# Chunk ends sent with K's transfers, a step fused, the exponential table first, weights held three pieces ahead, the first groups reordered

## The chip, the cores and the metric

The kernel runs on one core of a Trainium2 chip. The metric is the device time of one execution in microseconds (us). Three runs of the kernel before took 955.64, 958.70 and 959.11 us, median 958.7. Further down, TensorE (PE) multiplies matrices, VectorE (DVE) and ScalarE (ACT) do the elementwise work, and SyncE (SP) issues all DMA transfers, one after the other, from one queue.

## The reference

Three parts follow each other. The first is a linear attention with complex decay, for 4 batches, 8 heads, 768 steps and 48 dimensions:

```
scale = min(|a|, 0.999) / (|a| + 1e-6);  a = a * scale          # a complex, per step and dimension
for t in range(S):
    S_re, S_im = a[t] * (S_re + i S_im);  S_re += outer(k[t], v[t])
    y[t] = q[t] @ S_re
```

The second and third work on the 3,072 tokens of y, with 384 columns each:

```
h = x @ w_in;  x2 = (h * clip(h + 3, 0, 6) / 6) @ w_out         # 384 -> 2048 -> 384
out = (((x2 @ w1) * (x2 @ w2)) @ w3) @ w_out2                   # 384 -> 1024 -> 1024 -> 384
```

The weights come as 64-bit numbers, and are turned into 32-bit ones on the chip.

## The kernel before

The sequence is cut into chunks of 128 steps, 6 in a batch, 24 in all. Two chunks make a group, and `group(gi)` does for a group what doesn't need the state: from a_re and a_im (tiles ar and ai, 128x768) the logarithm of the magnitude and the angle; a running product of the magnitudes within a chunk (L534, into s, called G in the code) and a running sum of the angles (L540, into ai, called th); then sine and cosine of the angle (tile cs), and K and Q multiplied by them (Kc, and cs again). In that layout a dimension lies across partitions and heads together, so six DMAs bring Kc into KT and six bring cs into QT, 96 partitions of one head each (L584). `chunk(u)` transposes Kc on TensorE (L634, into Ks by ScalarE copies), updates the state A (L669), forms the scores (L643), masks them on VectorE (into P), and multiplies them with v and the state (L655, L660); the result goes to ys. Six DMAs bring ys into xh or xf (L602). For the state's update the magnitude at each chunk's end is needed in KT's layout. Before, it was copied out of G into ge (L563) and brought to a small tile mt by six DMAs of 1 KB (L566):

```
DVE(0.17, lambda: dve.tensor_copy(out=ge(), in_=G()[:, :, 127:TG:128]), [G], [ge])
```

The second part runs in blocks of 2, 2, 4, 4, 4, 4 and 4 chunks. For each of 16 slices f of the 2,048 columns, `s1` multiplies by w_in and ScalarE and VectorE apply the nonlinearity, and `s2` multiplies by w_out and adds up in three accumulators m. Block 0 does it with whole fp32 matmuls (called native here, L806 and L837); from block 1 on each operand is split into a high and a low fp32r part and each product takes three matmuls (L681 to L683). This part has its weights in 16 pieces of 768 columns (wiT and woT in turn). Each is decoded by one ScalarE and three VectorE steps (L695 to L698); for block 1 it is split by one step of each.

All this is not issued in the order in which it is written. Every operation is recorded with an estimated duration, its operands, and buffers from pools; `Plan.run` then acts out the engines and puts the operations into an order for each of them: among those that can start, the one with the earliest due time less its boost. Due times are counted back from pins, times given to the matmuls of the second and third parts; the list UB and the lists in `step` give boosts to single groups. The order is fixed when the program is built. A switch of ScalarE's function table (L1068) is put in when the next operation needs the other set: `EXP_SET` for Ln and Exp, `TRIG_SET` for Arctan and Sin; `hold` is added to the key of an operation that would need a switch. The pools matter as well: SyncE issues in order, so a load that waits for its buffer, or for a decode (`decode` lets the load of piece n wait for the decode of piece n - AHEAD), holds up what is queued behind it. After the second part the weights of the third are folded and the third part runs; the change doesn't touch that.

Of the kernel before, what the change touches and what calls it, by code (L numbers as in the profile page):

```python
# [7 lines left out]
F32 = mybir.dt.float32  # L8
F32R = mybir.dt.float32r
I32 = mybir.dt.int32  # L10
U64 = mybir.dt.uint64
BF16 = mybir.dt.bfloat16
# [38 lines left out]
class Plan:  # L51
# [52 lines left out]
    def run(self, swap, engines=("PE", "ACT", "DVE", "SP", "POOL"), window=48, switch=1.3, hold=4.0):  # L104
# [19 lines left out]
        table, bus, cols = None, 0.0, {}  # L124
# [29 lines left out]
        while len(order) < n:  # L154
# [60 lines left out]
            if o.size:  # L215
                bus = max(bus, o.end + 0.65) + o.size / 360e3
                o.lat = bus + 1.55 - o.end
# [34 lines left out]
def c_m4(n):  # L252
    return 2 * (n / 1200.0 + 0.015)


def c_mm(n):
    return n / 2400.0 + 0.016
# [145 lines left out]
def main_kernel(tc, q, k, v, a_re, a_im, w_in, w_out, w1, w2, w3, w_out2, consts, qT, kT, arT, aiT, vT, wiT, woT, w1T, w2T, w3T, wo2T, out, blocks=(2, 2, 4, 4, 4, 4, 4)):  # L403
# [16 lines left out]
    groups = [(b, c0, GT) for b in range(B) for c0 in range(0, CPB, GT)]  # L420
# [5 lines left out]
    with tc.tile_pool(name="keep", bufs=1) as kp:  # L426
      c5_ = kp.tile([128, 2, 128], F32, name="c2")
      flag = kp.tile([1, 1], I32, name="flag")
      with ctx:
# [28 lines left out]
        gall = fixed([128, NG, KD, GT], "gall")  # L458
# [13 lines left out]
        mG, mT = fixed([128, N], "mG", BF16), fixed([128, N], "mT", BF16)  # L472
# [10 lines left out]
        def DMA(fn, r, w, size, **kw):  # L483
            return P.add("SP", 0.55, lambda: fn(nc.sync), r, w, lat=2.2 + size / 360e3, size=size, **kw)
# [15 lines left out]

        xbuf = {}
# [4 lines left out]
        def group(gi):  # L506
            b, c0, C = groups[gi]
            g = c0 // GT
            cA, cT, cS = c_act(N), c_tt(N), c_ts(N)
            first, last = c0 == 0, c0 + C == CPB  # L510

            def nb(name, shape=None, n=1, tag=None):
                return SB(tag or name, shape or [128, KD, TG], BUFS.get(tag or name, n))
            ar, ai, kk, qq = (nb(n) for n in ("ar", "ai", "k", "q"))
            for t_, src in ((ar, arT), (ai, aiT), (kk, kT), (qq, qT)):
                DMA(lambda e, t_=t_, src=src: e.dma_start(out=flat(t_), in_=src[b, g]), [], [t_], 393216)
# [17 lines left out]
            DVE(2 * N / 960.0 + 0.15, lambda: dve.tensor_tensor_scan(out=flat(G), data0=mG.ap, data1=flat(G), initial=1.0, op0=ALU.max, op1=ALU.mult), [], [G])  # L534
            DVE(0.17, lambda: dve.tensor_copy(out=gall.ap[:, gi], in_=G()[:, :, 127:TG:128]), [G], [])
# [4 lines left out]
            DVE(2 * N / 960.0 + 0.15, lambda: dve.tensor_tensor_scan(out=flat(th), data0=mT.ap, data1=flat(th), initial=0.0, op0=ALU.mult, op1=ALU.add), [], [th])  # L540
            n_ = nb("u")
            ACT(cA, lambda: A(n_().bitcast(I32), th(), AF.Copy, scale=INV2PI), [th], [n_])
            ACT(cA, lambda: A(th(), th(), AF.Copy, scale=INV2PI), [], [th])
            DVE(cT, lambda: TT(th(), th(), n_().bitcast(I32), ALU.subtract), [n_], [th])
            if not last:
                ce = nb("ce", [128, KD], 2)
                DVE(0.17, lambda: dve.tensor_copy(out=ce().unsqueeze(2), in_=th()[:, :, TG - 1:TG]), [th], [ce])
                A_prev["ce"] = ce
            cs = nb("cs", [128, 2, KD, TG])
            ACT(cA, lambda: A(cs()[:, 0], th(), AF.Abs), [th], [cs])  # L550
            mt = nb("mt", [96, H, GT], 2)
            ge = nb("ge", [128, KD, GT], 2)
# [10 lines left out]
            DVE(0.17, lambda: dve.tensor_copy(out=ge(), in_=G()[:, :, 127:TG:128]), [G], [ge])  # L563
            for a in range(2):
                for t in range(KD):
                    DMA(lambda e, a=a, t=t: e.dma_start(out=mt()[48 * a + t:48 * a + 48:KD], in_=ge()[:, t, :]), [ge], [mt], 60000, part=True)  # L566

# [5 lines left out]
            Kc = nb("Kc", [128, 2, KD, TG])  # L573
            KT, QT = nb("KT", [96, H, TG]), nb("QT", [96, H, TG])

            def prod(o, f):
                for a in range(2):
                    TT(o()[:, a], cs()[:, a], f(), ALU.mult)
            DVE(2 * cT, lambda: prod(Kc, kk), [cs, kk], [Kc])

            def regroup(dst, src, w):
                for a in range(2):
                    for t in range(KD):
                        DMA(lambda e, a=a, t=t: e.dma_start(out=dst()[48 * a + t:48 * a + 48:KD], in_=src()[:, a, t, :]),  # L584
                            [src], [dst], 800 * w, part=True)
            regroup(KT, Kc, TG)
            DVE(2 * cT, lambda: prod(cs, qq), [qq], [cs] + ([ready0] if gi == 0 else []))
            regroup(QT, cs, TG)
            ys = nb("ys", [128, 4, C, 128])
            for c in range(C):  # L590
                chunk(b * CPB + c0 + c, c, Kc, KT, QT, ys, mt)
# [3 lines left out]
            if j < NATIVE:  # L595
                xf = SB("xh", [128, KD, NMAX], 1, F32R)
                xbuf[j] = (xf, xf, xf, xf)
            else:
                xf = nb("xf", [128, KD, TG])
            for i in range(KD):  # L600
                for e_ in range(2):
                    DMA(lambda e, i=i, e_=e_: e.dma_start(out=xf()[64 * e_:64 * e_ + 64, i, :TG].bitcast(F32), in_=ys()[64 * e_ + i:64 * e_ + 48:KD].rearrange("e p c t -> e p (c t)")),  # L602
                        [ys], [xf], 100000, part=True)
            if j < NATIVE:
                return
            if j not in xbuf:
                if j == 1:
                    w = SB("W", [128, 2, KD, TG], NW, F32R, 1, "alt")
                    xbuf[j] = (w, w, lambda w=w: w()[:, 0], lambda w=w: w()[:, 1])
                else:  # L610
                    h_, l_ = SB("xh", [128, KD, NMAX], 1, F32R), SB("xl", [128, KD, NMAX], 1, F32R)
                    xbuf[j] = (h_, l_, h_, l_)
            bh, bl, xh, xl = xbuf[j]
            o = (u - blk[j][0]) * 128
            ACT(cA, lambda: A(xh()[:, :, o:o + TG], xf(), AF.Copy), [xf], [bh], part=True)
            DVE(cT, lambda: TT(xl()[:, :, o:o + TG], xf(), xh()[:, :, o:o + TG].bitcast(F32), ALU.subtract), [xf, bh], [bl], part=True)

        def chunk(u, c_, Kc, KT, QT, ys, mt):
# [45 lines left out]
            if not last:  # L664
                pu = PS("x", [96, H, D], 5, 1)

                def upd():
                    for h in range(H):
                        pe.matmul(pu()[:, h, :], Ks()[:, h, :], vb.ap[:, h, 0:D])  # L669
                An = At[u % 2]  # L670
                PE(8 * 0.164 + 0.1, upd, [Ks, vb], [pu, An])
                mb = lambda: mt()[:, :, c_:c_ + 1].to_broadcast([96, H, D])
                o_ = An.ap[:, :, 0:D]
                if first:
                    DVE(c_tt(384), lambda: TT(o_, pu(), mb(), ALU.mult), [pu, mt], [An])
                else:
                    DVE(c_tt(384), lambda: TT(o_, pu(), Ap.ap[:, :, 0:D], ALU.add), [pu, Ap], [An])
                    DVE(c_tt(384), lambda: TT(o_, o_, mb(), ALU.mult), [mt], [An])
# [13 lines left out]
        def to32(raw, words, n, dst, ov):  # L692
# [3 lines left out]
            DVE(c_ts(n), lambda: dve.tensor_scalar(out=words(0), in0=words(0), scalar1=29, scalar2=None, op0=ALU.logical_shift_right), [raw], [lo_])  # L696
# [18 lines left out]
        EARLY, AHEAD = 4, 5  # L715
        taken_up = []

        def decode(src, i, after=()):
# [5 lines left out]
            taken_up.append(to32(raw, words, 768, raw, f))  # L724
# [10 lines left out]
        T0, att, GAP, GAP1 = 70.0, 2.97, 0, 0.0  # L735
        pins = {}
        t_ = 70.0
        first = 2
        for j, (a, n) in enumerate(blk):
            sl = 18 * c_mm(n * 128) + 3 * n / KF  # L740
            if 0 < j < first:
                d = sl * 7 * 1.47
                for f in range(KF):
                    pins["1", j, f] = pins["1", 0, f] + d
                    pins["2", j, f] = pins["2", 0, f] + d
                t_ += d
                continue
            if j == 0:
                sl *= 0.67
            for f in range(KF):  # L750
                pins["1", j, f] = t_
                pins["2", j, f] = t_ + 4.09 * sl
                t_ += sl
# [10 lines left out]
        def setup():  # L764
# [7 lines left out]
            dve.memset(mT.ap[:, 0:N:TG], 0.0)  # L772

        MB = 23.84
        NATIVE = 1
# [3 lines left out]
        def s1(j, f):  # L779
            n = blk[j][1] * 128  # L780
            fr = 1 if j < 2 else 0
# [43 lines left out]
        def s2(j, f, g, acc, at, own):  # L825
# [5 lines left out]
            def mm():  # L831
                kw = {"skip_group_check": True} if j < 2 else {}
# [18 lines left out]
        APART = 1  # L851

        UB = (23.1, 6.3, 0, 0, 0.7, 0)

        def step(u):
            US = (0, 0, 4.6)
# [31 lines left out]
        first = 2  # L888
        for js in [range(first)] + [[j] for j in range(first, len(blk))]:
# [5 lines left out]
            at = {j: i * TG for i, j in enumerate(js)}  # L895
            gs = {}
            if js[0] >= 3:
                j = js[0]
                for i in range(4):
                    stage(*todo.pop(0), [seen[blk[j][0] + 2 - i]], pins["1", j, 0] - 30 + 15 * i)  # L900
            lag = 7
            for st in range(KF + 2 + lag * (len(js) - 1)):
                for i, j in enumerate(js):
                    if 0 <= st - i * lag < KF:
                        gs[j, st - i * lag] = s1(j, st - i * lag)
                for i, j in enumerate(js):
                    if 0 <= st - i * lag - 2 < KF:
                        s2(j, st - i * lag - 2, gs.pop((j, st - i * lag - 2)), acc, at[j], own[j])
# [157 lines left out]
        with tc.manual_schedule():  # L1066
            setup()
            P.run(lambda t_: act.preload_act_table_set(t_), window=48, hold=2.24)  # L1068
            n0 = NG * KD * GT
            ok = sb.tile([128, n0 + 5 * NG], F32, tag="cs", name="cs", bufs=P.slots["cs"])  # L1070
            dve.tensor_scalar(out=ok[:, :n0], in0=gall.ap.rearrange("p g t c -> p (g t c)"), scalar1=1.1e-19, scalar2=None, op0=ALU.is_ge)
# [78 lines left out]
```

## Time and profile before

| | |
|---|---|
| runs | 955.64, 958.70, 959.11 us; median 958.7 |
| profiled execution | 963.3 us, its span 961.1 us |
| TensorE busy | 898.6 us (93%) |
| VectorE busy | 592.7 us (62%) |
| ScalarE busy | 495.1 us (52%) |
| mean granted clock of TensorE | 0.987 of 2.4 GHz |
| transfers | 102.87 MB, 107 GB/s on the mean |

The shares are means over stages of different kinds. In the first fifth of the span the two elementwise engines are nearly full and TensorE has holes; in the last two fifths it is the other way round. What an engine waits for has to be read by stretches. In the rows, x and m are accumulators, W is the pool of weight buffers, u and s are scratch tiles. The time of a row's instruction and the distance to the next one on the same engine may differ a little, since a step begins while the one before still drains.

### The profile page before, as it was taken

The numbers are of one execution on the slowest core, as the hardware profiler recorded it, in microseconds if no ns is written. First come the engines' busy times: TensorE is split into PE (matmuls) and PEld (weight loads), VectorE is DVE, ScalarE is ACT, GpSimd is POOL, SyncE is SP. The second block draws the span as 40 slices with busy tenths as digits, with TensorE's granted clock in tenths as the row PEclk, the third lists the DMA queues.
The fourth block names the chain that finished last, engine by engine and source line by source line (L and its number), as shares of the span: only waits on it lengthen the run. The fifth ranks groups of instructions, "written<-read, shape, count | busy, mean of one in ns | idle before, by whom it ended". The sixth has DMA issues, their size and how long they took to land.

```text
span 961.1 us, 13166 instructions
## 1 busy us (share of the span) xinstructions
PE 898.6 (93%) x5082; PEld 772.0 (80%) x5082; DVE 592.7 (62%) x914; ACT 495.1 (52%) x790; POOL 0.2 (0%) x4
## 2 busy tenths in 40 slices
PE   0578988999999999999999999999999999999996
PEld 0467887988877887888788888798888888888885
DVE  6998988899988669757563558974232323222221
ACT  7984976888869285837342446643221322121221
POOL 0000000000000000000000000000000000000000
PEclk9988999999999999999999999999999999999999
DMA  6575367163781347334255427531020101000001
GB/s 256 147 286 176 86 133 219 36 160 94 188 230 29 104 133 218 95 83 129 89 106 133 142 90 266 214 112 42 1 66 1 66 1 44 1 34 0 26 9 37
DMA packets 66742, 102.87 MB, mean 107 GB/s; under 512 B 17136, under 2 KB 44912, under 8 KB 66672
## 3 DMA queue, kind: packets, MB, share of 16 engines
q1 hardware_dynamic: 66672, 101.95, 35.9%
q8 instruction: 42, 0.69, 0.3%
q14 instruction: 28, 0.23, 0.1%
HBM read 64.62 MB, written 13.63 MB: 81 GB/s over the span
## 4 chain that ended last, share of the span: by engine, by line
PE 63%; DVE 14%; DMA 8%; ACT 7%; SPq 4%; issue 2%; DVEq 0%; ACTq 0%
PE x L681 10%; PE x L682 10%; PE x L683 10%; PE m L682 4%; PE m L683 4%; PE m L681 4%; PE m L1032 3%; PE m L1030 3%; PE m L1031 3%; SPq L584 3%; PE x L643 2%; ACT u L487 2%; DMA W<-in_w3T_dram 2%; DMA QT<-cs 2%; ACT L1068 1%
## 5 line engine op out<-in xcount | busy, mean ns | idle before, releaser
L487 ACT ACTIVATE r<-x 128x512 f32<-128x512 f32 (+1 forms) x144 | 81.7, 570 | 167.1 <-PE x L683 130.6
L490 DVE TENSOR_TENSOR r<-r,x 128x512 f32<-128x512 f32 x48 | 33.0, 688 | 179.3 <-PE x L683 179.3
L681 PE MATMUL m<-gh,W 128*128 128x512 f32 (+1 forms) x288 | 110.9, 385 | 1.9 <-ACT gh L487 1.8
L682 PE MATMUL m<-gl,W 128*128 128x512 f32 (+1 forms) x288 | 109.5, 380 | 1.4 <-DVE gl L490 1.1
L683 PE MATMUL m<-gh,W 128*128 128x512 f32 (+1 forms) x288 | 108.7, 378 | 0.0
L487 ACT ACTIVATE gh<-r 128x512 fp32r<-128x512 f32 (+1 forms) x96 | 56.7, 591 | 81.9 <-PE m L683 77.3
L681 PE MATMUL x<-xh,W 128*128 128x512 f32 x240 | 97.5, 406 | 0.1
L682 PE MATMUL x<-xl,W 128*128 128x512 f32 x240 | 95.0, 396 | 0.1
L683 PE MATMUL x<-xh,W 128*128 128x512 f32 x240 | 94.9, 396 | 0.0
L490 DVE TENSOR_TENSOR gl<-r,gh 128x512 fp32r<-128x512 f32 (+1 forms) x96 | 61.4, 642 | 49.9 <-ACT gh L487 48.4
L681 PE MATMUL x<-W 128*128 128x512 f32 (+1 forms) x228 | 84.7, 371 | 0.1
L682 PE MATMUL x<-W 128*128 128x512 f32 (+1 forms) x228 | 84.1, 369 | 0.0
L683 PE MATMUL x<-W 128*128 128x512 f32 (+1 forms) x228 | 84.0, 369 | 0.0
L819 DVE SCALAR_TENSOR_TENSOR r<-r,x 128x512 f32<-128x512 f32 (+1 forms) x96 | 61.0, 638 | 25.9 <-ACT r L487 24.8
L487 ACT ACTIVATE W<-W 128x768 f32<-128x768 f32 (+2 forms) x65 | 53.4, 833 | 27.7 <-DMA W<-in_w3T_dram 8.0
L682 PEld LDWEIGHTS m<-gl,W 128*128 128x128 f32 x288 | 54.6, 190 | 14.3 <-DVE gl L490 4.1
L681 PEld LDWEIGHTS m<-gh,W 128*128 128x128 f32 x288 | 54.6, 190 | 13.2 <-ACT gh L487 2.7
L683 PEld LDWEIGHTS m<-gh,W 128*128 128x128 f32 x288 | 54.6, 189 | 10.4
L643 PE MATMUL x<-QT,KT 96*128 96x128 f32 x384 | 53.9, 298 | 6.4 <-DMA QT<-cs 5.0
L643 PEld LDWEIGHTS x<-QT,KT 96*128 96x128 f32 x384 | 51.6, 212 | 9.0 <-issue 4.0
L487 ACT ACTIVATE u<-r 128x512 fp32r<-128x512 f32 x36 | 22.8, 633 | 63.7 <-DVE r L490 63.7
L681 PEld LDWEIGHTS x<-xh,W 128*128 128x128 f32 x240 | 45.1, 188 | 10.9 <-issue 1.0
(205 smaller groups left out, 1914.6 us busy)
## 6 DMA issues: line engine op xcount, KB each, us to landing
KT<-Kc SPq DMA_DIRECT2D x72, 128.0 KB, 3.5
QT<-cs SPq DMA_DIRECT2D x72, 128.0 KB, 3.6
W<-in_w3T_dram SPq DMA_DIRECT2D x16, 512.0 KB, 4.9
v<-in_vT_dram SPq DMA_DIRECT2D x24, 256.0 KB, 3.2
W<-in_wiT_dram SPq DMA_DIRECT2D x8, 768.0 KB, 7.0
W<-in_woT_dram SPq DMA_DIRECT2D x8, 768.0 KB, 8.0
ar<-in_arT_dram SPq DMA_DIRECT2D x12, 384.0 KB, 3.4
ai<-in_aiT_dram SPq DMA_DIRECT2D x12, 384.0 KB, 3.6
```

The costliest lines, as they stand in the source:

```text
L487: act.activation(out=o, in_=i, func=f, scale=scale, bias=bias, **kw)
L490: dve.tensor_tensor(out=o, in0=i0, in1=i1, op=op)
L584: DMA(lambda e, a=a, t=t: e.dma_start(out=dst()[48 * a + t:48 * a + 48:KD], in_=src()[:, a, t, :]), [src], [dst], 800 * w, part=True)
L643: pe.matmul(p_()[:, i, :], KT()[:, 4 * g + i, tok], QT()[:, 4 * g + i, tok])
L681: pe.matmul(o, wh, xh, start=start, stop=False, **kw)
L682: pe.matmul(o, wh, xl, start=False, stop=False, **kw)
L683: pe.matmul(o, wl, xh, start=False, stop=stop, **kw)
L819: DVE(c_tt(n), lambda: dve.scalar_tensor_tensor(out=r()[:, :n], in0=r()[:, :n], scalar=6.0, in1=h()[:, :n], op0=ALU.min, op1=ALU.mult), [h ...
L1030: pe.matmul(o, gh()[:, a], Wb()[:, 0, i % 2], start=(i == 0), stop=False)
L1031: pe.matmul(o, gh()[:, a], Wb()[:, 1, i % 2], start=False, stop=False)
L1032: pe.matmul(o, gl()[:, a], Wb()[:, 0, i % 2], start=False, stop=(i == KI - 1))
L1068: P.run(lambda t_: act.preload_act_table_set(t_), window=48, hold=2.24)
```

## The change

- The magnitudes at the chunks' ends are copied into two extra columns at the end of each row of Kc (which is now 258 wide), and travel in KT's six transfers; ge, mt and mt's transfers are gone. The state's update reads KT.
- The angle's scaling by 1/(2 pi), a ScalarE step over th, is fused into VectorE's subtraction that follows it.
- `Plan.run` gets `first`, with which the exponential table is loaded as the first thing on ScalarE.
- `AHEAD`, the number of weight pieces that may be loaded ahead of the decode, is 3 in place of 5.
- The planner's costs, pins and boosts are others (transfers at 300 in place of 360 GB/s, `hold` 5.2 in place of 2.24), so that the order is another one throughout, above all in the first four groups.
- Groups of one chunk, and a decode with its shift on ScalarE (`eased`), could now be chosen, but the tables that choose them name none.

```
-    def run(self, swap, engines=(...), window=48, switch=1.3, hold=4.0):
+    def run(self, swap, engines=(...), window=48, switch=1.3, hold=4.0, first=None):
-        table, bus, cols = None, 0.0, {}
+        table, bus, cols = first, 0.0, {}
+        if first:
+            swap(first)
...
-                bus = max(bus, o.end + 0.65) + o.size / 360e3
+                bus = max(bus, o.end + 0.65) + o.size / 300e3
...
             ACT(cA, lambda: A(n_().bitcast(I32), th(), AF.Copy, scale=INV2PI), [th], [n_])
-            ACT(cA, lambda: A(th(), th(), AF.Copy, scale=INV2PI), [], [th])
-            DVE(cT, lambda: TT(th(), th(), n_().bitcast(I32), ALU.subtract), [n_], [th])
+            DVE(cT, lambda: STT(th(), th(), INV2PI, n_().bitcast(I32), ALU.mult, ALU.subtract), [n_], [th])
...
-            DVE(0.17, lambda: dve.tensor_copy(out=ge(), in_=G()[:, :, 127:TG:128]), [G], [ge])
-            for a in range(2):
-                for t in range(KD):
-                    DMA(lambda e, a=a, t=t: e.dma_start(out=mt()[48 * a + t:48 * a + 48:KD], in_=ge()[:, t, :]), [ge], [mt], 60000, part=True)
...
+            def ends():
+                for a in range(2):
+                    dve.tensor_copy(out=Kc()[:, a, :, w:], in_=G()[:, :, 127:w:128])
+            DVE(0.3, ends, [G], [Kc])
...
-                mb = lambda: mt()[:, :, c_:c_ + 1].to_broadcast([96, H, D])
+                mb = lambda: KT()[:, :, mt:mt + 1].to_broadcast([96, H, D])
...
-        EARLY, AHEAD = 4, 5
+        EARLY, AHEAD = 4, 3
...
-        APART = 1
-        UB = (23.1, 6.3, 0, 0, 0.7, 0)
+        APART = 4
+        UB = (23.1, 3.6, 0, 0, 10.9, 5.2)
...
-            P.run(lambda t_: act.preload_act_table_set(t_), window=48, hold=2.24)
+            P.run(lambda t_: act.preload_act_table_set(t_), window=48, hold=5.2, first=EXP_SET)
```

The order of the new program moves at many places. Three are shown. The first is ScalarE from the program's start: s and ar, ai belong to the first group, W is a weight piece. Before:

```order
L487 ACT_TABLE_LOAD
L487 ACTIVATE s_117,rsum<-ar 128x768
L487 ACTIVATE u<-ai 128x768
L1068 ACT_TABLE_LOAD
L487 ACTIVATE u<-s_117 128x768
```

And now:

```order
L1092 ACT_TABLE_LOAD
L491 ACTIVATE s_121,rsum<-ar 128x768
L491 ACTIVATE u<-ai 128x768
L491 ACTIVATE u<-s_121 128x768
L491 ACTIVATE u<-u 128x768
```

The load between the two squares and the first Ln is gone; the one at the start is now that of the exponential set.

The second is SyncE's queue where the first group's K and Q are sent. Before:

```order
L516 DMA k<-in_kT_dram 128x768
L584 DMA KT<-Kc 16x8x256 x6
L584 DMA QT<-cs 16x8x256 x6
L566 DMA mt<-ge 16x8x2 x6
L516 DMA ar<-in_arT_dram 128x768
L689 DMA W<-in_wiT_dram 128x768
L516 DMA q<-in_qT_dram 128x768
L689 DMA W<-in_woT_dram 128x768
```

And now:

```order
L541 DMA k<-in_kT_dram 128x768
L606 DMA KT<-Kc 16x8x258 x6
L606 DMA QT<-cs 16x8x256 x6
L541 DMA q<-in_qT_dram 128x768
L713 DMA W<-in_wiT_dram 128x768
L713 DMA W<-in_woT_dram 128x768
L541 DMA ar<-in_arT_dram 128x768
L650 DMA v_71<-in_vT_dram 128x512
```

The six transfers of mt have gone from between QT and the weights.

The third is ScalarE around the second group's sine and cosine (cs<-ai and cs<-cs behind a table load); ys<-x are the copies of the first group's two results. Before:

```order
L487 ACTIVATE ys<-x 128x4x128
L487 ACTIVATE u<-u 128x768
L487 ACTIVATE W<-W 128x768 x3
L487 ACTIVATE ar<-ar 128x768
L487 ACTIVATE W<-W 128x768
L1068 ACT_TABLE_LOAD
L487 ACTIVATE cs<-ai 128x768
L487 ACTIVATE cs<-cs 128x768
```

And now:

```order
L1092 ACT_TABLE_LOAD
L491 ACTIVATE cs<-ai 128x768
L491 ACTIVATE cs<-cs 128x768
L491 ACTIVATE ys<-x 128x4x128
L491 ACTIVATE u<-u 128x768
L491 ACTIVATE W<-W 128x768 x2
L491 ACTIVATE s_371,rsum<-ar 128x768
L491 ACTIVATE W<-W 128x768
L491 ACTIVATE ys<-x 128x4x128
```

The sine and cosine stood behind both copies ys, the second of which is the first row above; now they stand ahead of both.

## Rows read from the trace of the kernel before

**Rows 1.** The page: each engine's busy time, share of the span, instructions

```profile
PE 898.6 (93%) x5082; PEld 772.0 (80%) x5082; DVE 592.7 (62%) x914; ACT 495.1 (52%) x790; POOL 0.2 (0%) x4
```

**Rows 2.** Stretches: length, busy time of PE, PEld, DVE, ACT, POOL; clock; DMA

```profile
62.80:184.80 122.00, 113.29 (x818) 102.95 (x819) 108.82 (x172) 83.89 (x143) 0.00 (x0) 0.93 0.50 140
184.80:580.00 395.20, 392.27 (x2346) 323.66 (x2345) 288.64 (x440) 242.31 (x382) 0.00 (x0) 1.00 0.46 125
580.00:955.00 375.00, 371.88 (x1798) 326.80 (x1796) 143.31 (x223) 114.66 (x195) 0.00 (x0) 1.00 0.16 56
...
20.00:160.00 140.00, 112.61 (x777) 101.64 (x779) 130.14 (x201) 105.58 (x164) 0.00 (x0) 0.94 0.56 160
```

**Rows 3.** TensorE in order of time: start, length; in brackets idle time before

```profile
30.17 1.77 PE L634 MATMUL x<-c,Kc 128*128 128x128 f32 x6 [30.17 <-DVE Kc L490]
...
62.84 5.53 PE L806 MATMUL x<-xh,W 128*128 128x256 f32 x18 [6.67 <-DMA xh<-ys]
...
79.84 3.75 PE L643 MATMUL x<-QT,KT 96*128 96x128 f32 x16 [2.71 <-DMA QT<-cs]
...
90.76 1.95 PE L643 MATMUL x<-QT,KT 96*128 96x128 f32 x16
...
129.70 1.28 PE L643 MATMUL x<-QT,KT 96*128 96x128 f32 x8 [2.27 <-DMA QT<-cs]
...
168.05 4.54 PE L806 MATMUL x<-xh,W 128*128 128x256 f32 x12 [3.01 <-ACT ys L487]
...
184.84 0.48 PE L681 MATMUL x<-xh,W 128*128 128x512 f32 x1
```

**Rows 4.** The chain that ended last, in order of time: start, length

```profile
7.36 1.28 ACT L1068
...
14.94 0.47 DVE W L696
...
17.07 1.66 DVE ai L540
...
21.75 0.73 ACT ai L487
...
68.94 1.74 DVE cs L490 x2
...
76.44 2.95 DMA QT<-cs
```

**Rows 5.** VectorE in order of time, first group

```profile
29.15 1.82 DVE L490 TENSOR_TENSOR Kc<-cs,k 128x768 f32<-128x768 f32 x2 [0.16 <-ACT cs L487]
...
31.77 0.16 DVE L563 COPY ge<-s 128x6 f32<-128x6 f32 x1
```

**Rows 6.** Groups by shape: count, busy us, mean ns, idle before

```profile
L698 DVE SCALAR_TENSOR_TENSOR W<-W 128x768 int32<-128x768 int32 x28 | 26.6, 952 | 0.0
```

**Rows 7.** SyncE's queue in order of time: start, length, transfers

```profile
39.52 3.83 SPq L566 DMA_DIRECT2D mt<-ge  x6
...
44.03 0.43 SPq L689 DMA_DIRECT2D W<-in_wiT_dram  x1
...
58.01 3.81 SPq L602 DMA_DIRECT2D xh<-ys  x6
```

**Rows 8.** Transfers by line: count, KB of each, median us to landing

```profile
KT<-Kc SPq DMA_DIRECT2D x72, 128.0 KB, 3.5
...
W<-in_woT_dram SPq DMA_DIRECT2D x8, 768.0 KB, 8.0
```

**Rows 9.** ScalarE in order of time: the second group's sine

```profile
63.86 0.84 ACT L487 ACTIVATE cs<-ai 128x768 f32<-128x768 f32 x1
```

**Rows 10.** Waits from 0 to 190 us: total, times, longest

```profile
SPq L602 <- DVE xl L490: 11.5, 1, 11.5
...
ACT W L487 <- DMA W<-in_woT_dram: 5.3, 2, 4.5
...
DVE P L490 <- PE x L643: 5.0, 8, 1.5
```

## What was predicted

> **What bounds the kernel now.** The page's engine shares come first: the reader is to see TensorE at 93% of the span [rows 1], so the end moves only by TensorE's work, its idle time and its slow clock. The change leaves the matmuls alone: both programs hold 4,838 rows of TensorE. The table by stretches says where TensorE is not full [rows 2]: from 184.8 to 580 us it lacks 395.20 - 392.27 = 2.9 us, from 580 to 955 us 3.1 us, but from 62.8 to 184.8 us 8.7 us, and there its mean granted clock is 0.93. VectorE is busy 130.1 of 140 us from 20 to 160 us, so the early order is mostly a question of what VectorE does first. TensorE's timeline names the losses [rows 3]: nothing before 30.17 us; 6.67 us for the first group's result xh; 2.71 and 2.27 us for QT; 3.01 us where a ScalarE copy came late. After such holes the clock is at the lower of its two levels: the 16 score matmuls at 79.84 us took 3.75 us, the same 16 at 90.76 us 1.95 us. Block 2, from which on TensorE nearly always has work, begins at 184.84 us. What can be won lies before that.
>
> **The change part by part, on the path.** I walk the new order by hand with the durations of the rows.
>
> *The head.* Before, a table load of 1.28 us stands between the squares and the first Ln [rows 4]. Now that table is loaded first, while ar is still in flight: -1.28 us. VectorE's decode step ahead of the scans goes: -0.47. So the scan of the angles, over at 18.73, is over at 17.0. From there ScalarE does a copy, a load, Ln, Abs, Exp, a square of the next group and the square that VectorE waits for, 6.0 us as before (Abs now stands where the scaling copy ai<-ai stood): 23.0. VectorE then has four steps of 0.87 (0.95 long, 0.08 of it under the next), the end copies and q: 23.0 + 3.5 + 0.25 + 0.87 = 27.6. There Kc starts, which before waited for the sine until 29.15 [rows 5]. Its first half is done at 28.5, and the first transposes start at 28.7: 1.5 us of the 30.17.
>
> The end copies have no row; the nearest is the ge copy that they replace, 0.16 us [rows 5]. Two of them cost nothing (in the shadow of the step before) to 0.4 us a group; I take 0.25, against 0.1 saved: 12 x 0.15 = 1.8 us on VectorE in all, hidden in its idle time once block 2 has begun. The fused subtract costs what the plain one did: all steps of 768 columns and two inputs stand near 0.95 us [rows 6]. The ScalarE step that goes is 0.73 us, 12 x 0.73 = 8.8 us. The new plan makes 34 table loads in place of 29: 5 x 1.28 = 6.4 us. ScalarE's total so falls by 2.4 us, nothing of it on the path after 185 us, where ScalarE is idle 39% [rows 2]. Before that two loads more (2.6) stand against four copies less (2.9): nothing.
>
> The row shows a load as 1.28 us on the path, with the next row 0.01 us behind it. The Trainium skill, page "ScalarE: Activation LUTs", section "What ACT_TABLE_LOAD costs", adds a drain of about 1.38 us to each switch, 2.66 us in all; by that the two loads more would cost 5.3 against the 2.9, and if all of it lay on the path the time would be 2.4 us longer than I forecast. The trace doesn't bear it out here.
>
> *The queue.* Six mt transfers take the queue 3.83 us a group [rows 7], 72 of them 46 us. The first six stand in front of the weight loads, which therefore leave from 44 us on. Now these loads stand right behind QT and q, about 6 us earlier; they land some 8 us after issue [rows 8]. KT's rows grow from 1,024 to 1,032 bytes: no row shows the price. From below 0; from above KT's landing, 3.5 us, doubled. QT's six transfers are issued behind KT's for another 4 us and the scores need both, so even the upper end is covered; without the cover it is 3.5 us a group. I take 0. The state update now waits for KT in place of mt, which was queued behind QT: not later.
>
> *To the first native matmul.* Of the head's 1.5 us little is left: the updates wait for ScalarE's Ks, and the masks stand behind two angle steps of the next group on VectorE, so the first group's second result comes at 55.8 us. The queue sends xh at 56.5 us in place of 58.01 [rows 7], and the first native matmul starts at 62.0 in place of 62.84, with 1.1 us of the second group's transposes done before it: 2.0 us.
>
> *The next groups.* In the order before, the second group's sine stands behind two copies ys and about a dozen other ScalarE steps; it began at 63.86 us [rows 9]. Now it stands ahead of both ys, at 49.1. Its products are then held by VectorE alone: cs is done at 63.7 (before 68.94 + 1.74 = 70.7) and QT lands at 72.5 (before 76.44 + 2.95 = 79.4) [rows 4]. The scores start at 73.4, straight behind the fourth native step, without the wait of 2.71 us and the slow clock after it. For the third group I get cs at 105.3, QT at 112.7 and no wait (before, scores at 129.70 after 2.27); for the fourth QT at 150.8. The native matmuls find their weights (last decode at 167.5, used at 167.6). Block 2 starts at 174.7. Between 62 us and there my walk leaves TensorE four waits of 0.3 to 1.2 us, 2.3 together.
>
> *Sum.* Block 2 now has work in front that before came later, 27 matmuls at 0.119 us and an update of 1.3: 4.5 us. 184.84 + 4.5 = 189.3 against 174.7 is a gain of 14.6. The other way round, from the losses: 2.0, then 8.7 - 2.3 = 6.4 of idle time, then the slow clock, 0.07 x 122 = 8.5 us less about 2.6 for the restart behind xh, which stays: 2.0 + 6.4 + 5.9 = 14.3. But the walk has VectorE at 98% for the 164 us from 10 to 174; it did 93% [rows 2]. At 95% the same work takes 164 x 0.98/0.95 = 169.2, 5.2 us more. That is my choice between two ends: no drift (-14.6), and the share of before (8.8 us more, and 3 of slow clock in the holes that this makes: -2.8). I take -14.6 + 5.2 = -9.4, and leave the 6 us of later waits as they are. Profiled: 963.3 - 9.4 = 953.9. That execution is 4.6 us above the median of the three runs, 958.7, so the median is **949.3 us**.
>
> **The rivals.**
> *VectorE takes it all back.* Its share was 0.93 with the old order, and the new one asks for the same products and decodes sooner. By the end above the gain is 2.8: 956 us. For it: in the walk the decodes of 46 to 53 us already delay the scores' masks. Against it: much of VectorE's idle time was in waits for what other engines bring (5.0 us for the scores alone, [rows 10]), which the new order moves forward.
> *The loads held three ahead block the queue (slower).* A load now waits for the decode three pieces back, not five, and all that is behind it on SyncE waits too: behind the eleventh to fourteenth load stand xf, KT and QT of the third and fourth groups. In my walk these loads are free 2 to 10 us before those products are. It decides from the point where the decode step is later than the product. The longest queue wait of this stage was 11.5 us [rows 10]. With 4 us of native work to cover it and 1.9 us of slow clock after it (3.75 against 1.95 on the scores), at both groups: 2 x (11.5 - 4 + 1.9) = 18.8, with the 5.2 above and less 14.6: +9.4, 968 us. ScalarE's wait of 4.5 us for one weight piece [rows 10] speaks for it; that with five ahead the same loads were the ones waited for, so that the number ahead was not what held them, against.
> *The gain is given back late.* After 184.8 us TensorE lost 6.0 us. The planner has reordered there as well. Twice those losses: -9.4 + 6 = -3.4, 955 us. For it: five more table switches. Against it: VectorE is busy only 73% there.
>
> **How the numbers follow.** The forecast has 0.60, VectorE taking it back 0.19, the late loss 0.08, the blocked queue 0.13. Within 0.5%, about what a measurement can't tell from no change, means 953.9 to 963.5. So faster 0.60, same 0.27, slower 0.13. The likeliest case's own range is 943 to 954 (from no drift to twice mine). The range to hold 8 in 10 takes in both small cases and the lesser half of the blocked queue: 942 to 964.
>
> **What would show it.** Right: a table load ahead of the first square and none before the first Ln; first transposes at 28 to 29.5 us; on the queue QT's issue followed by q and loads, with no mt; the second group's sine before the first ys, at 49 to 52 us; its scores at 72 to 76 us with no wait; block 2 from 175 to 183 us; TensorE idle under 5 us from 62 us to there; 34 loads of 1.28 us. Wrong: block 2 at 185 us or later with VectorE over 95% busy (first rival); a load's wait on SyncE over 5 us with QT behind it (second); more than 8 us idle on TensorE after block 2 has begun (third). A first native matmul later than 63 us would make the head's part wrong.

## The result and the profile after

The changed kernel takes 943.4 us (median of 4 runs, 941.99 to 945.72); the kernel before, beside it on the same chip, 958.9 (4 runs). The ratio is 0.9845, with a 95% interval of 0.9811 to 0.9879. Forecast were 949.3 us and a range of 942 to 964. The gain is 15.5 us by the medians (14.8 by the ratio) where 9.4 were forecast.

The spans of the two profiled executions differ by more than the medians, 21.3 us: that of before (963.3 us) was longer than each of its timed runs, that of the changed kernel (941.99) the shortest of four. So up to 6 us of what the two traces show between them may belong to these executions and not to the change. The page of the changed kernel, engine shares:

```profile
span 939.8 us, 13065 instructions
...
PE 888.5 (95%) x5082; PEld 765.6 (81%) x5082; DVE 593.7 (63%) x928; ACT 490.0 (52%) x783; POOL 0.2 (0%) x4
```

TensorE's busy time falls by 10.1 us against [rows 1] and its idle time by 11.2 (span less busy time: 62.5 before, 51.3 now): no matmul is gone (5,082 in both), and the mean granted clock is 0.994 in place of 0.987, so more of them ran at the higher level. The stretches say where (length, busy time of PE, PEld, DVE, ACT, POOL; clock; DMA):

```profile
20.00:160.00 140.00, 116.22 (x851) 104.44 (x852) 134.90 (x214) 112.33 (x176) 0.00 (x0) 0.98 0.64 175
62.80:174.00 111.20, 106.64 (x838) 97.84 (x837) 107.46 (x178) 84.30 (x141) 0.00 (x0) 1.00 0.58 155
...
200.00:580.00 380.00, 380.00 (x2272) 314.77 (x2271) 283.09 (x438) 232.00 (x366) 0.00 (x0) 1.00 0.48 135
580.00:935.00 355.00, 352.29 (x1717) 311.85 (x1715) 125.00 (x195) 99.96 (x171) 0.00 (x0) 1.00 0.14 46
```

Against [rows 2]: VectorE went from 130.14 to 134.90 us busy of the same 140, the clock between 62.8 us and block 2 from 0.93 to 1.00. From 200 to 580 us TensorE has no gap that the profile shows. The rows of TensorE that answer to [rows 3]:

```profile
28.05 1.77 PE L658 MATMUL x<-c,Kc 128*128 128x128 f32 x6 [28.05 <-DVE Kc L494]
...
58.22 1.75 PE L658 MATMUL x<-c,Kc 128*128 128x128 f32 x6 [6.08 <-DVE Kc L494]
59.76 2.56 PE L832 MATMUL x<-xh,W 128*128 128x256 f32 x6
...
71.05 2.02 PE L667 MATMUL x<-QT,KT 96*128 96x128 f32 x16 [0.74 <-DMA QT<-cs]
...
113.72 2.02 PE L667 MATMUL x<-QT,KT 96*128 96x128 f32 x16 [2.19 <-DMA q<-in_qT_dram]
...
174.98 0.39 PE L705 MATMUL x<-xh,W 128*128 128x512 f32 x1
```

Block 2 starts at 174.98 us, before at 184.84. Between 62.8 us and there TensorE now lacks 4.6 us (111.20 - 106.64).

ScalarE (start, length), the table load of the first group and the second group's sine, against [rows 9]:

```profile
16.25 0.85 ACT L491 ACTIVATE u<-ai 128x768 int32<-128x768 f32 x1 [1.67 <-DVE ai L565]
17.11 1.28 ACT L1092 ACT_TABLE_LOAD   x1
18.40 0.84 ACT L491 ACTIVATE u<-s 128x768 f32<-128x768 f32 x1
...
47.53 0.84 ACT L491 ACTIVATE cs<-ai 128x768 f32<-128x768 f32 x1
```

A load is 1.28 us with its neighbours 0.01 us away on either side. That doesn't bear out the drain that the Trainium skill, page "ScalarE: Activation LUTs", section "What ACT_TABLE_LOAD costs", adds to each switch.

SyncE's queue, against [rows 7]: behind QT stand q and the weight loads, no mt.

```profile
33.31 3.77 SPq L606 DMA_DIRECT2D QT<-cs  x6
37.12 0.59 SPq L541 DMA_DIRECT2D q<-in_qT_dram  x1
37.75 0.46 SPq L713 DMA_DIRECT2D W<-in_wiT_dram  x1
...
54.02 3.81 SPq L626 DMA_DIRECT2D xh<-ys  x6
```

### The profile page after: what moved, and what is told of

The parts are those of the page before. It is cut to its first block, busy times and chain, and to the rows that moved or that the text cites. A ratio compares the mean times of both kernels' runs of the same rounds, so it can differ in the third digit from the quotient of the medians.

```text
span 939.8 us, 13065 instructions
## 1 busy us (share of the span) xinstructions
PE 888.5 (95%) x5082; PEld 765.6 (81%) x5082; DVE 593.7 (63%) x928; ACT 490.0 (52%) x783; POOL 0.2 (0%) x4
## 3 DMA queue, kind: packets, MB, share of 16 engines
q1 hardware_dynamic: 56304, 101.94, 37.5%
## 4 chain that ended last, share of the span: by engine, by line
PE 87%; DVE 5%; ACT 4%; DMA 2%; SPq 1%; issue 0%; DVEq 0%; ACTq 0%
PE x L705 14%; PE x L707 13%; PE x L706 13%; PE m L705 7%; PE m L707 6%; PE m L706 6%; PE x L667 4%; PE m L1056 3%; PE m L1054 3%; PE m L1055 3%; PE x L693 2%; PE x L679 2%; ACT u L491 2%; PE x L684 2%; PE m L1007 1%; PE m L1006 1%
## 5 line engine op out<-in xcount | busy, mean ns | idle before, releaser
L705 PEld LDWEIGHTS x<-xh,W 128*128 128x128 f32 x240 | 45.2, 188 | 11.2 <-issue 1.4
L707 PEld LDWEIGHTS x<-xh,W 128*128 128x128 f32 x240 | 45.2, 188 | 11.0
L667 PE MATMUL x<-QT,KT 96*128 96x128 f32 x384 | 49.9, 285 | 3.5 <-DMA q<-in_qT_dram 2.8
```

The lines of the kernel that those rows point to most:

```text
L667: pe.matmul(p_()[:, i, :], KT()[:, 4 * g + i, tok], QT()[:, 4 * g + i, tok])
L705: pe.matmul(o, wh, xh, start=start, stop=False, **kw)
L707: pe.matmul(o, wl, xh, start=False, stop=stop, **kw)
```

## The experiments

Where an edit is undone or added "in what is issued", the order is the one planned for the kernel that it is made in; only the instructions themselves differ. Differences are differences of the ratios, times 958 us. Theory to begin with: the new order brings most of the gain, the three edits a little each.

**Ends in K, table first and scaling copy dropped, in the old order** (the core of the diff against the kernel before; a small copy on GpSimd, out of KT, lets the old readers of mt stand):

```diff
-    DMA(... out=mt()[48 * a + t:48 * a + 48:KD], in_=ge()[:, t, :] ...)
+    dve.tensor_copy(out=o()[:, a, :, TG:], in_=kept[0])   # into Kc
+    nc.gpsimd.tensor_copy(out=mt(), in_=KT()[:, :, TG:])
+swap(EXP_SET)                                             # ahead of all
-A(th(), th(), AF.Copy, scale=INV2PI)
```

> The kernel before with the three edits (ends in K's transfers, the scaling step gone, the exponential table first), in the old order: the planner sees the old program, only what is issued differs. Theory A, the order is what gains: the edits alone bring 3 to 6 us of the 15.5 (1.3 to 2 at the head, the rest from weights that leave 3.8 us earlier), so 953 to 956 us, and TensorE still waits for QT at the second group's scores (about 77 to 79 us) and has its late waits near 278, 303 and 613 us. Theory B, the edits gain and the order only follows them: 10 us or more, 949 us or less, with the wait at the second group's scores gone.

Measured: 953.73 us, ratio 0.9962 [0.9946, 0.9977], -3.6 us. The time is as theory A has it; the 1.3 to 2 us at the head are not there. The first transposes come at 29.62 us (30.17 before, 29.84 with the ends alone, further down). ScalarE reaches the first Ln at 6.33 us, in the run with the ends alone at 7.75, but then, in order of time, stands still for the first weight piece, whose decode this order puts ahead of the Arctan that VectorE waits for:

```profile
13.09 0.93 ACT L490 ACTIVATE W<-W 128x768 f32<-128x768 f32 x1 [1.63 <-DMA W<-in_wiT_dram]
```

In the new order that decode stands behind the Arctan. Nor were the scaling copy's 0.73 us awaited here: Kc starts at 28.61 us straight behind VectorE's own steps, without a wait for the sine.

**The new order alone**, the three edits undone in what is issued, mt's six transfers right behind QT's:

```diff
 regroup(QT, cs, w)
+for a_ in range(2):
+    for t_ in range(KD):
+        e.dma_start(out=mt()[48 * a_ + t_:48 * a_ + 48:KD], in_=ge()[:, t_, :])
-swap(first)
+A(th(), th(), AF.Copy, scale=INV2PI)
```

> The changed kernel with the three edits undone in what is issued (mt sent by six transfers behind QT's, the scaling step back on ScalarE, the exponential table loaded where it is needed), in the new order. Theory A: it keeps 9 to 12 of the 15.5 us, 947 to 950 us; no late waits of TensorE beyond 1 us after block 2 has begun, the first transposes near 30 us. Theory B: it keeps 5 us or less, 954 us or more.

Measured: 968.94 us, ratio 1.0121 [1.0098, 1.0143]: 11.6 us slower than before. The theory falls. The edits alone give -3.6, the order alone +11.6, both together -14.8.

**mt back, alone**, in the new order (the loop of the diff above, with the ge copy and K's rows of 256 columns that go with it; the other two edits stand):

> The changed kernel, with mt sent by six small transfers behind QT's again, in the new order. Theory A: the queue is not what held TensorE in the new order, +0 to 2.5 us, 943.5 to 946 us. Theory B: the 3.8 us of queue a group come back at two groups or more, +5 us or more, 948.5 us or more.

Measured: 961.86 us, ratio 1.0045 [1.003, 1.006]: 19.2 us above the changed kernel. VectorE's longest item in the waits up to 190 us (total, times, longest):

```profile
DVE A L494 <- DMA mt<-ge: 18.1, 4, 5.7
```

The first of these waits, in VectorE's order of time (start, length; in brackets the idle time before):

```profile
36.58 0.95 DVE L741 SCALAR_TENSOR_TENSOR W<-W 128x768 int32<-128x768 int32 x1
42.00 0.55 DVE L494 TENSOR_TENSOR A<-x,mt 96x384 f32<-96x384 f32 x1 [4.47 <-DMA mt<-ge]
42.48 1.74 DVE L559 TENSOR_TENSOR_SCAN s<-mG,s 128x768 f32<-128x768 bf16 x1
```

In the same timeline SyncE's queue and TensorE's first matmul of block 2:

```profile
36.93 3.80 SPq L622 DMA_DIRECT2D mt<-ge  x6
...
191.59 0.40 PE L721 MATMUL x<-xh,W 128*128 128x512 f32 x1
```

The new order has the state update A due on VectorE at 37.5 us; mt leaves the queue at 40.7. VectorE works in order, so what stands behind A (the scans of the next group, the masks, the decodes) waits as well. Four such waits make 18.1 us; block 2 comes 16.6 us later. In the changed kernel, VectorE in order of time, the same A finds its ends with K:

```profile
36.72 0.95 DVE L725 SCALAR_TENSOR_TENSOR W<-W 128x768 int32<-128x768 int32 x1
37.59 0.55 DVE L494 TENSOR_TENSOR A<-x,KT 96x384 f32<-96x384 f32 x1
```

In the kernel before, VectorE in order of time, the order asked for A later:

```profile
44.62 0.55 DVE L490 TENSOR_TENSOR A<-x,mt 96x384 f32<-96x384 f32 x1 [0.35 <-DMA mt<-ge]
```

So mt cost VectorE next to nothing there. From the waits of that kernel from 0 to 190 us (total, times, longest; the first is of use further down):

```profile
DVE r L819 <- ACT r L487: 3.9, 3, 2.5
...
DVE A L490 <- DMA mt<-ge: 1.5, 2, 1.2
```

**Loads held five ahead**, planned anew (`EARLY, AHEAD = 4, 3` to `4, 5`):

> The changed kernel with AHEAD 5 in place of 3, planned anew. My second rival said that a load waits for the decode three pieces back. The trace of the changed kernel speaks against a wait on the chip: loads leave before that decode. If the number only moves the planner's order, the time is within 3 us of 943.4, either way, with the order after the first four groups alike. If holding three is what gave TensorE its weights in time, 947 us or more, with waits of the native matmuls for decodes.

Measured: 944.74 us, ratio 0.9867 [0.9845, 0.9889], +2.1 us with overlapping intervals. No difference is shown. In the changed kernel the eleventh load leaves at 68.84 us, the decode step of the eighth piece that it should follow starts at 76.25. So the number shapes the plan; it made no wait on the chip.

Now the new question: is it VectorE's wait for mt, or the 3.8 us of queue a group? Two kernels are to part them.

**Six unread transfers behind QT**, the ends still in K:

```diff
+mt = sb.tile([96, H, GT], F32, tag="mt", name="mt", bufs=2)
+e.dma_start(out=mt[48 * a_ + t_:48 * a_ + 48:KD], in_=src()[:, a_, t_, :GT])   # six, read by nobody
```

> The changed kernel, with six more transfers of 8-byte rows behind QT's in each group, of a size and a place in the queue as mt's had, into a tile that nobody reads; chunk ends still come with K. Theory A (what cost the 18.5 us of 'mt put back' is VectorE standing still for mt's landing, 18.1 us in four waits, with masks and K's products queued behind): no reader, so no wait; 943 to 947 us, VectorE waits for KT under 1 us. Theory B (it is the 3.8 us of queue a group, which makes weights and loads late): as late as with mt back, 957 to 963 us.

Measured: 952.26 us, ratio 0.9933 [0.9916, 0.995]: +8.4 us, between the two theories. The trace parts the time before block 2 from the time after. TensorE's first matmul of block 2, in order of time:

```profile
176.10 0.39 PE L714 MATMUL x<-xh,W 128*128 128x512 f32 x1
```

and the stretch from 200 to 580 us (columns as above):

```profile
200.00:580.00 380.00, 374.04 (x2242) 308.29 (x2241) 274.83 (x424) 226.12 (x357) 0.00 (x0) 1.00 0.47 132
```

Block 2 is only 1.1 us late (16.6 with mt read): up to there theory A holds, VectorE waits 0.2 us for KT. But later TensorE lacks 6.0 us where it lacked none, waiting for masks and other VectorE results. That is not shown to be the price of the queue's length, for this edit does one thing that mt did not: mt was read from ge, and these transfers read cs (60 of the 72) or Kc (12), so that the next sine and the next end copies wait until they have landed. Waits from 195 to 580 us, ScalarE's and VectorE's (total, times, longest):

```profile
ACT cs L491 <- DMA mt<-cs: 10.3, 3, 4.4
...
DVE Kc L599 <- DMA mt<-Kc: 4.7, 2, 2.5
```

In the changed kernel the sine waited 2.6 us there, for QT. With mt back, sent from ge on as long a queue, it waited 2.2 us and TensorE lacked only 0.9 us; but there all was 16.6 us late already. So of the 8.4 us some 7 come after block 2 has begun, and whether they are the queue's or those of the tiles that were held longer stays open; a run that sends the six from a tile of their own would tell.

**mt ahead of QT**: the same six transfers, read, but sent between K's and Q's:

```diff
+if len(sent) == 7:   # before QT's first
+    ... e.dma_start(out=mt()[48 * a_ + t_:48 * a_ + 48:KD], in_=ge()[:, t_, :])
```

> The changed kernel's order with mt's six transfers back, sent ahead of QT's and not behind them. The queue is as long as with mt behind QT (961.9 us), mt lands 3.8 us earlier, QT as much later. Theory A (VectorE's wait for mt): the first update, due at 37.6 us, finds mt at about 38.5, so the four waits of 4.5 us shrink to 0 to 1.5 us each; instead the scores wait for QT 1 to 4 us a group in some groups; 947 to 956 us. Theory B (queue time): no different from mt behind QT, 959 to 964 us.

Measured: 968.79 us, ratio 1.0112 [1.0096, 1.0129], slower than either theory had it. The waits up to 190 us (total, times, longest):

```profile
DVE P L494 <- PE x L683: 8.3, 6, 4.2
...
DVE A L494 <- DMA mt<-ge: 2.9, 2, 2.0
...
PE x L683 <- DMA QT<-cs: 10.2, 3, 4.4
```

The wait for mt shrank from 18.1 to 2.9 us, as A says; the scores' wait for QT took its place, and VectorE then waited for the scores. Theory A's price for this (1 to 4 us in some groups) was too small: block 2 starts at 190.0 us, and the stretch from 200 to 580 lacks 6.0 us as with the unread transfers. There too the sine waits 10.3 us, here for QT's transfers, which read cs later. Neither of the two places tried in this queue was free for six more transfers.

**The table loaded where it is needed** in the new order:

```diff
-if first:
-    swap(first)
+shown = None   # and swap at the first Ln
```

> The changed kernel with the first table loaded where Ln needs it. Theory A (1.28 us on the head's chain, and TensorE has too little idle time behind it to win it back): first transposes 1.3 us later, 944.3 to 946 us. Theory B (VectorE's and SyncE's timetable has no room, a late head costs several times itself): 947 us or more. Theory C (hidden): within 0.5 us of 943.4.

Measured: 946.91 us, ratio 0.9875 [0.9858, 0.9893], +2.9 us (3.5 by the medians). The interval overlaps that of the changed kernel, so the size is not shown; by the median it lies between theories A and B. The trace (of the slowest of the four runs, 949.24 us) shows that the load is not hidden: 1.6 us at the head have become 3.3 at block 2, TensorE in order of time:

```profile
29.63 1.77 PE L659 MATMUL x<-c,Kc 128*128 128x128 f32 x6 [29.63 <-DVE Kc L495]
...
66.40 4.02 PE L833 MATMUL x<-xh,W 128*128 128x256 f32 x12
...
178.29 0.39 PE L706 MATMUL x<-xh,W 128*128 128x512 f32 x1
```

The twelve native matmuls at 66.40 us took 4.02 us; in the changed kernel the twelve at 63.60 took 2.82. From 63 to 68 us the granted clock was 0.50 here and 1.00 there (the 1.2 and the 2.4 GHz level), TensorE having been busy 3.68 of the 5 us before, there 4.78. That is 1.2 of the 1.7 us of growth, in one execution.

**The scaling copy back** in the new order:

```diff
+A(th(), th(), AF.Copy, scale=INV2PI)
-STT(th(), th(), INV2PI, n_().bitcast(I32), ALU.mult, ALU.subtract)
+TT(th(), th(), n_().bitcast(I32), ALU.subtract)
```

> The changed kernel with the scaling copy on ScalarE back (0.73 us, 12 times) and a plain subtract on VectorE. Theory A (the prediction: ScalarE has room, net nothing): 943 to 945 us. Theory B (with the early order VectorE's subtract waits for two ScalarE steps instead of one, at the head and in each early group, and the step stands ahead of the sine): 0.7 to 1.5 us for each of the first three groups, 946 to 950 us; with mt back both edits undone together cost 7.1 us, which speaks for it.

Measured: 948.60 us, ratio 0.9902 [0.9886, 0.9918], +5.5 us: the time is theory B's. The first transposes come at 30.02 us (+2.0), the second group's at 60.75 (+2.5), block 2 at 179.57 (+4.6). Not all of it is the copy's: in this execution ai landed later, and ScalarE took it at 6.85 us in place of 5.76, which is 1.1 of the 2.0 us at the head. What is left grows by steps of the copy's size, 0.9 and 1.4 us at the first two groups, which fits 0.73 us for each early group but does not show it. The three edits undone one by one cost 19.2 + 2.9 + 5.5 = 27.6 us, all at once 26.4: in the new order they add up, within the intervals.

**The ends in K alone, in the old order** (the first three lines of the first diff):

> The kernel before, in its own order, with mt's six transfers gone and the chunk ends sent in K's rows; tables and the scaling copy as before. In the old order VectorE waited for mt only 1.5 us up to 190 us. Theory A (mt's price is the wait of VectorE in the new order, so without the new order its going is worth little): 955.5 to 958.4 us, 0 to 3 us less than before. Theory B (queue time is worth the same in any order; six unread transfers cost the changed kernel 8.4 us): 949 to 952 us.

Measured: 954.48 us, ratio 0.9956 [0.9939, 0.9973], -4.2 us: between the theories, and as much as all three edits together gave in that order (-3.6). There the two ScalarE edits are worth nothing that shows. What mt's going gives is, at one place at least, queue time: in the order before, the second group's mt stands ahead of its KT. SyncE's queue in order of time, before:

```profile
65.08 3.82 SPq L566 DMA_DIRECT2D mt<-ge  x6
69.02 4.14 SPq L584 DMA_DIRECT2D KT<-Kc  x6
```

and in this run:

```profile
67.02 3.84 SPq L595 DMA_DIRECT2D KT<-Kc  x6
```

KT leaves 2.0 us sooner, 0.75 of them because Kc was begun sooner (66.02 against 66.77 us), and TensorE's wait of 2.71 us for QT [rows 3] is gone (1.30 us are left, for another operand of VectorE's). The later stage gains nothing from the shorter queue here: from 200 to 580 us TensorE lacks 4.1 us, 2.9 before.

Two tries at a better kernel. **Two swaps at the head**, in what is issued: q's scaling behind K's products, the awaited square ahead of the next group's:

```diff
-TT(qq(), qq(), G(), ALU.mult); prod(Kc, kk)
+prod(Kc, kk); TT(qq(), qq(), G(), ALU.mult)
-A(G(), ar(), AF.Square ...)   # second group; then A(sq(), y(), AF.Square), first group
+A(sq(), y(), AF.Square)       # then the second group's
```

> The changed kernel with two swaps in what is issued: on VectorE q's scaling behind K's products (in every group) instead of ahead of them; on ScalarE the square that VectorE waits for at the head ahead of the second group's first square. Theory A (a delay at the head of 1.3 to 2 us came out 2 to 3 times as long in 'table undone' and 'scaling copy back', so an earlier head is worth as much): first transposes at about 26.5 us in place of 28.05, second group's at 56.5 to 57.4 in place of 58.22, 940 to 942.5 us. Theory B (TensorE is already at 96% from 62.8 us on, an earlier head finds no slack to use): 942.5 to 944.5 us. Slower only if K's transfers, sent earlier, get into the way of the loads ai and k: above 945 us.

Measured: 943.52 us, ratio 0.985 [0.9831, 0.9869]: theory B. The transposes come 1.0 us earlier in both groups, and nothing is left of it. TensorE in order of time:

```profile
27.05 1.77 PE L680 MATMUL x<-c,Kc 128*128 128x128 f32 x6 [27.05 <-DVE Kc L494]
32.08 2.16 PE L715 MATMUL x<-v,Ks 128*96 128x48 f32 x12 [3.25 <-ACT Ks L491]
...
174.75 0.39 PE L727 MATMUL x<-xh,W 128*128 128x512 f32 x1
```

The update behind the transposes waits for ScalarE's Ks, which did not move. In these runs a late head cost time, and an earlier one won none.

**One decode step of the first eight pieces on ScalarE**, planned anew:

```diff
-EASED = range(0, 0)
+EASED = range(0, 8)
```

> The changed kernel, planned anew with one step of the decoding of the first eight weight pieces on ScalarE (0.73 us each) instead of VectorE (0.47 us each). VectorE is at 96% from 20 to 160 us, ScalarE at 80%. Theory A (VectorE is what binds the early stage): VectorE has 3.8 us less to do before 60 us, block 2 starts 2 to 4 us earlier, 939 to 942 us. Theory B (the head binds, through ScalarE as much as VectorE: every added ScalarE step there delays the chain): 944 to 949 us.

Measured: 941.80 us, ratio 0.9833 [0.9814, 0.9852], block 2 at 173.52 us. In the direction of theory A, and the lowest median of all; its interval overlaps that of the changed kernel, so it isn't shown to be faster.

## Why the prediction was right, and where not

*The bound and the place.* Right. TensorE's work stayed, and what was won before block 2 was won where the stretches had shown gaps and the low clock.

*The head.* Forecast 28.7 us for the first transposes and 62.0 for the first native matmul; they came at 28.05 and 59.76. Right in kind. About 0.8 us of the 2.1 at the first transposes is luck, since the first input landed sooner in the execution after. ScalarE's first square in order of time, before:

```profile
5.54 0.84 ACT L487 ACTIVATE s<-ar 128x768 f32<-128x768 f32 x1 [3.51 <-DMA ar<-in_arT_dram]
```

and after:

```profile
4.68 0.84 ACT L491 ACTIVATE s<-ar 128x768 f32<-128x768 f32 x1 [2.66 <-DMA ar<-in_arT_dram]
```

*The walk through the groups.* Sine 47.53 (49.1), scores 71.05 with a wait of 0.74 (73.4 without), block 2 174.98 (174.7). The walk was right to 0.3 us at its end, but not on the way: the first native matmul, the sine and the scores came 1.6 to 2.4 us early (the sine and the scores ahead of the stretches named as signs), and TensorE then waited 4.6 us where the walk had 2.3, 2.19 of them ahead of the third group's scores, where it had none.

*The sum.* Here failed the term that I set against the walk: "it did 93% [rows 2]. At 95% the same work takes 164 x 0.98/0.95 = 169.2, 5.2 us more." Block 2 came 0.3 us after the walk's time, not 5.2. The share itself was well chosen; the stretch of the walk, columns as above:

```profile
10.00:174.00 164.00, 130.22 (x978) 117.83 (x979) 156.93 (x250) 131.76 (x206) 0.00 (x0) 0.98 0.62 177
```

VectorE was busy 156.93 of 164 us, 95.7% (and from 20 to 160 us 96.4%, 93% before). But it was not the same work: 98% of 164 is 160.7 us, 3.8 more than VectorE did up to there. The walk had put too much work and too few waits in front of block 2, and the two nearly cancelled. That is luck, and the 5.2 us put right only one of the two. Which steps the walk had too much is not on record. VectorE's waits from 20 to 190 us (total, times, longest) show what is left:

```profile
DVE u L494 <- ACT u L491: 2.5, 2, 1.9
DVE P L494 <- PE x L667: 1.8, 3, 1.3
DVE gl L494 <- ACT gh L491: 1.4, 2, 1.0
DVE gh L841 <- ACT gh L491: 0.4, 1, 0.4
DVE A L494 <- DMA KT<-Kc: 0.2, 1, 0.2
```

The wait for the scores fell from 5.0 us [rows 10] to 1.8, the wait for mt from 1.5 to 0.2 for KT, and the 3.9 us for ScalarE's r are gone. The old share was no property of VectorE but these waits, and the argument that the new order moves them forward stood in the text, as a reason against the first rival. The second term off was "leave the 6 us of later waits as they are": 2.7 are left, none of them between 174 and 580 us. What took them away is not shown. A shorter queue alone is not it, since the old order without mt lacked 4.1 us from 200 to 580 us, and the new order with mt only 0.9. The two terms, 4.9 and 3.3 us, make 8.2, more than the 5.9 us between 949.3 and 943.4; the rest lies within the 6 us by which the two profiled executions differ beyond the medians.

*The state update* "now waits for KT in place of mt, which was queued behind QT: not later" was true of the first group (the second group's mt stood ahead of KT) and priced at nothing. It is what the walk stood on. In the new order the update comes 7 us earlier (37.59 against 44.62 us); read from mt it would have waited 18.1 us in four groups. I had followed the wait of before and not asked what the same transfer costs the new order.

*ScalarE net nothing* was wrong as a statement on parts: in the new order the copy is worth 5.5 us by its run, and the table 2.9, which is within the intervals; both stand on the chain of the first groups. It did no harm to the sum, as the walk had used the durations themselves.

*K's longer rows.* 0, as taken. Landing (KB of each, median us to landing):

```profile
KT<-Kc SPq DMA_DIRECT2D x72, 129.0 KB, 4.2
QT<-cs SPq DMA_DIRECT2D x72, 128.0 KB, 4.3
```

KT rose from 3.5 us [rows 8], but QT, whose rows are as before, rose from 3.6 to 4.3; with mt back and rows of 1,024 bytes KT landed in 4.1.

*The rivals.* VectorE took nothing back. The blocked queue did not happen as described, since the number ahead made no wait on the chip. (Its 1.9 us of slow clock is 1.8 by the two rows that it names, 3.75 and 1.95, and its sum 18.6.) The later stage gave some time rather than took it. But a slower outcome was closer than any of the three said: the new order without the ends in K is 11.6 us slower than before once the other two edits are out as well, and 4.3 slower by itself.

What stays open: the 4.2 us of the ends in the old order were followed to the second group's KT and no further; what the new order does to the later stage was not traced; and the unread transfers price the queue and the held tiles together.

## What to carry to other kernels

A new order and the edits that come with it are priced together: ask of every transfer that is shortened or merged when its reader is now due, not when it was. A wait on an engine that works in order delays everything behind it (18.1 us of waits brought block 2 16.6 us later), so look at the queue in front of the operand. A transfer also holds the tile that it reads until it has landed, so ask who writes that tile next. A low busy share is read through its waits before it is carried over to the new kernel: where the waits go, the share goes too.

## What the runs showed that I had not expected

Transfers of 8-byte rows that nobody reads, six in each of the 12 groups, 1 KB each, cost 8.4 us, only 1.1 of them before block 2; from 195 to 580 us the sine then waited 10.3 us for them to have read its tile. The last of mt's six lands about 1.3 us after the queue has issued it (issued by 40.73 us, VectorE goes on at 42.00). In single executions a delay of 1.6 and of 2.0 us at the head stood at 3.3 and 4.6 us by block 2 (the second with a copy in each later group too), and an advance of 1.0 us had shrunk to 0.2.
